# Feature group 2 on seven products for all four chunks, the last attention unit's sums on one engine, and another order in the output projection

## The chip, the cores and the metric

The kernel runs on one core of a Trainium2 chip. Its time is the device time of one execution in microseconds; the median of 3 runs of the kernel before is 745.07 us (744.22 to 745.59). One execution was also profiled, and took 744.5 us. In that profile the engines are called PE (TensorE, its matmuls), PEld (TensorE's weight loads), DVE (VectorE), ACT (ScalarE), POOL (GpSimd) and SP (SyncE, which here only issues transfers). L1190 is line 1190 of the kernel before.

## The reference

A gated layer over 2048 positions of 640 features. The input is normalised; one branch is attention over a dilated window of eight keys, followed by an output projection; the other is a bilinear unit, whose result goes through a silu and multiplies the first.

```python
B, S, D, F, H = 1, 2048, 640, 1536, 32        # Dh = 20, window W = 8, dilation 2
xn = layernorm(x)
q, k, v = split(xn @ wqkv)                    # 32 heads of 20
idx = pos[:, None] - arange(W) * 2            # masked where negative
attn = softmax(einsum("bhsd,bhswd->bhsw", q, k[idx]) * Dh ** -0.5)
s = einsum("bhsw,bhswd->bhsd", attn, v[idx]) @ wo
h = (xn @ w_gate) * (xn @ w_up)               # no nonlinearity on either branch
out = x + s * silu(h @ w_down)
```

## The kernel before

Every product is in single precision, made of three matmuls: each operand is split into a high part (a copy on ACT, L114) and a low part (a subtraction on POOL or DVE, L115), and high x high, high x low and low x high are summed in a bank of PSUM. The normalised input stands transposed in SBUF as four chunks of 512 positions (`xT`, tiles `xc`), and the 1536 features of the bilinear unit are twelve groups of 128.

The program goes through these stages. Products for q, k and v (`qkv`, L433) in blocks of heads, with attention's units following on DVE and POOL. Then feature groups 2 to 11 of the bilinear unit, while attention goes on. Then the output projection, and last the product with `w_down`. Each engine works through its own list in program order, so an instruction that waits holds up all that is behind it on its engine. The order is written out by hand: attention is a generator, and each call of `advance` after a piece of TensorE's work lets it emit as many of its pieces as the piece has credit for.

**Feature groups.** The gate and up products of one feature group over two chunks can be done as a Strassen-like scheme of seven products instead of eight (`group`, L1334): sums of blocks of the weights (S1, S2, S3, S4, d5, on POOL) meet blocks of the input (A11 and so on name the weights' blocks, B11, B21, B22 the input's) and sums of those, T1 to T4. For the chunks 2 and 3 the T tiles are made in SBUF during the q, k, v products (`differences`). For the chunks 0 and 1 they were made at the start and put away in DRAM (`t_scr`, `e_scr`), and come back by `load_t` (L1190, four loads of 768 KB) and `load_e` (L1194, two loads of 512 KB, over the first two rows of chunk 1), all issued from POOL's queue. `F_TWO` is the first feature group whose chunks 0 and 1 use them: 3. So group 2 does the chunks 2 and 3 by seven products, and the chunks 0 and 1 by plain products (`gate` and `up`, L124, 15 matmuls each). From group 3 to 10 each feature group is two calls of `group`. Within a call the products come in the order B11, B21, T2, T1, T3, B22, T4; ACT copies four of them into tiles `gh` (`hold`, L1303), and gate_b (L1306), up_b (L1309), h_b (L1312), gate_a (L1316) and up_a (L1319) combine them; `VEC` = 3 says from which group on up_b and h_b of the chunks 2 and 3 go to DVE instead of POOL. A tile `gh` comes free when its store to `h_scr` has landed; there are six.

**Attention's sums.** A unit has eight terms t = e * v on DVE (L503) and seven additions of them into o (L509), on POOL. Only in the last unit every second addition is on DVE.

**The last h.** `up` multiplies gate and up on DVE (L1378); the very last one is a copy on ACT (L1380) and a product on POOL (L1381). Its store is the last to `h_scr` ahead of the output projection, whose own `gh` tiles are laid where the old ones were.

**The output projection.** Five pairs of blocks of 128 positions by seven products each (`pair_product`, L1041), in the banks A, C, A, C, A, B, A; then six blocks by plain products (L124). ACT holds the products 0, 1 and 2 of a pair in `kept` (L1044); DVE adds product 3 (L1047), product 4 (L1050) and product 5 (L1052) to what was held. Product 6 goes on in bank A after product 4 has been read by L1050. Between them lie the splits of the next pair's input: `hi_pair` (L1016, ACT) and `lo_pair` (L1020, DVE). DVE also transposes blocks of o (L718) and makes sums of `w_down`'s blocks (L805, L808, L814, L817), whose splits run on ACT and POOL.

Of the kernel before, what the change touches and what calls it, by code (L numbers as in the profile page):

```python
# [13 lines left out]
AF = mybir.ActivationFunctionType  # L14
# [28 lines left out]
SP = 10  # L43
PAIRS = range(0, W, 2)
PACE = 1.0
VEC = 3
EARLY = 1
GROUP_RATE = 0.184

# [7 lines left out]
def kernel(  # L57
# [319 lines left out]

    UN = [(g, r) for g in range(len(GROUPS)) for r in range(DIL)]
    ORDER = [0, 1, 2, 3, 4, 6, 5, 7, 8, 11, 9, 10]
    wide, now = [], [None]  # L380
    q_t, kv_t, kv_buf, kv_zero, scr, staged, made = {}, {}, {}, {}, {}, [], set()

    def view_kv(u, b):
# [41 lines left out]
    def qkv(m, r, i, runs=ALL_RUNS, at=None, act=None, bank=("q", 3)):  # L425
# [9 lines left out]
        if m or r:  # L435
            if not staged:
                y = slot([P, 2, 2 * 3 * CMAX], F32)
                staged.extend([y[:, 0], y[:, 1], st([P, 2 * 3 * CMAX], "pk", 1)])
# [27 lines left out]
    def attention():  # L466
# [28 lines left out]
        def values(w):  # L495
# [6 lines left out]
            v = flat(kv_t[u][:, 1, w:w + NE, :]).rearrange("p (n d) -> p n d", d=DH)  # L502
            nc.vector.tensor_mul(t.rearrange("p (n d) -> p n d", d=DH),  # L503
                                 e[:, :, w].unsqueeze(2).to_broadcast([P, NE * nh, DH]), v)
# [866 lines left out]
    def up(f, ch, gs):  # L1371

        p = plain(f, 1, ch)

        def finish():
            hs = st([P, CH], "gh", 5)
            if (f, ch) != (f1, NCH - 1):
                nc.vector.tensor_mul(hs, p, gs)  # L1378
# [9 lines left out]
    def next_sums(f):  # L1388
        w_split(f, "S", "R")
        w_sum.pop(f)  # L1390
        if f < f1:
            load_wf(f + 1)

    def first_parts():
        for name in ("S1", "S2", "S3", "d5", "S4"):
            w_add(2, name)
            yield
        w_split(2, "S")
        yield
        w_split(2, "G")  # L1400
        yield

    steps += [differences(k) for k in range(2)]
# [3 lines left out]
    for m, t in ((m, t) for m in range(1, len(MADE)) for t in range(DIL)):  # L1407
# [3 lines left out]
        for i in range(NE):  # L1411
# [7 lines left out]
            if (m, r, i) == (last - 1, 1, 6):  # L1419
                load_wf(2)  # L1420
            qkv(m, r, i)
            if i == 1:
                finish_piece()
            advance(PACE * heads * 0.38)
# [29 lines left out]
                  (1, 2): splits("G"), (1, 4): splits("S"), (1, 5): splits("R"), (1, 6): splits("U")}  # L1454

    def load_late(n):
        if n < 2:
            load_t(n + 2)
        else:
            load_e(1, n - 2, n - 2)  # L1460

    for f in range(2, f1):
        places.clear()
        if not two(f):
            places.update({(0, 3): sums("S1", "S2"), (0, 4): sums("S3", "d5", "S4")})
# [6 lines left out]
            if two(f + 1):  # L1472
                tw.pop("G")
            w_split(f + 1, "G")
            up(f, 0, g0)
            up(f, 1, g1)
            if two(f + 1):
                tw.pop("U")
            continue
        places.update(two_places)  # L1480
        if f == F_TWO:
            places.update({(0, n): lambda f, n=n: load_late(n) for n in range(4)})
        group(f, 2)
        group(f, 0, 1)
    places.clear()
# [54 lines left out]
    pair_product(0, 0)  # L1540
    for p in range(SP // 2):
        more = p + 1 < SP // 2
        if not more:
            y1 = turn_o(SP)
        if p < 3:
            wd_sums()
        pair_product(p, 1)
# [14 lines left out]
        if more:  # L1562
            if p == 3:
                hi_pair(p + 1, 2)
            if p:
                lo_pair(p + 1, 2)
# [118 lines left out]
```

## Time and profile before

| what | value |
|---|---|
| median of 3 runs | 745.07 us |
| the profiled execution | 744.5 us |
| its span, first to last instruction | 742.7 us |
| PE busy | 734.2 us (99%) |
| DVE busy | 612.5 us (82%) |
| POOL busy | 463.5 us (62%) |
| ACT busy | 301.9 us (41%) |
| granted TensorE clock | 0.999 |

A view of the timeline has a row for each run of like instructions: start, length, engine, line, operation, what it writes and reads, how many; in brackets stands how long the engine was idle ahead of it and what ended that. The execution is 1.8 us longer than its span.

### The profile page before, as it was taken

To read this page: it belongs to the slowest core of one execution; us is meant where nothing else is said; L and a number is where in the kernel's file an instruction comes from. 1 tells how busy PE (TensorE), PEld (TensorE's weight loads), DVE (VectorE), ACT (ScalarE), POOL (GpSimd) and SP (SyncE) were. 2 spreads that over 40 slices of the span, in tenths; PEclk is the share of its full clock that TensorE was granted. 3 is DMA by queue.
4 is the path that set the end of the run, shared out by engine and by line. 5 is a ranking of instruction groups with operands and counts; after the bars stand their busy time and mean duration, and the time that the engine had idled before them with its cause. 6 is when DMAs were issued, how large, how long until landed. Compare 5 with 4: busy or idle time off the path is not lost. (4 is left out here: it accounts for less than half of the span.)

```text
span 742.7 us, 11094 instructions
## 1 busy us (share of the span) xinstructions
PE 734.2 (99%) x4054; PEld 669.7 (90%) x4054; DVE 612.5 (82%) x720; ACT 301.9 (41%) x577; POOL 463.5 (62%) x389
## 2 busy tenths in 40 slices
PE   9999999999999999999999999999999999999997
PEld 7989989988999998888888888888899999999997
DVE  7676998799687988999999998758898777777775
ACT  5668312322332332233232332235556564444442
POOL 6159919887688879798879889787558800000000
PEclk9999999999999999999999999999999999999999
DMA  8465582868355736863455244269457655555534
GB/s 326 164 202 175 220 268 87 247 212 248 97 175 152 232 105 216 286 193 110 154 132 177 75 123 119 64 180 264 126 160 215 232 218 192 192 192 192 192 107 142
DMA packets 103493, 132.98 MB, mean 179 GB/s; under 512 B 22696, under 2 KB 74404, under 8 KB 103438
## 3 DMA queue, kind: packets, MB, share of 16 engines
q1 hardware_dynamic: 86286, 114.25, 48.4%
q10 hardware_dynamic: 16000, 12.78, 5.3%
q0 software_dynamic: 1152, 5.24, 2.2%
q8 instruction: 32, 0.52, 0.3%
q14 instruction: 23, 0.19, 0.1%
HBM read 83.58 MB, written 47.81 MB: 177 GB/s over the span
## 5 line engine op out<-in xcount | busy, mean ns | idle before, releaser
L509 POOL TENSOR_TENSOR o<-o,t 128x960 f32<-128x960 f32 (+1 forms) x69 | 139.9, 2028 | 15.5 <-DVE t L503 14.2
L503 DVE TENSOR_TENSOR t<-e,kv 128x960 f32<-128x960 f32 (+1 forms) x96 | 99.6, 1039 | 23.3 <-POOL o L509 23.3
L535 DVE TENSOR_TENSOR t<-q,kv 128x1920 f32<-128x1920 f32 (+1 forms) x48 | 92.5, 1927 | 4.1 <-DMA kv<-qkv_scr 4.0
L542 DVE TENSOR_REDUCE lg<-t 128x96 f32<-128x1920 f32 (+1 forms) x48 | 92.3, 1923 | 0.2
L433 PE MATMUL q<-s,xc 128*128 128x360 f32 (+1 forms) x450 | 83.0, 334 | 0.0
L115 POOL TENSOR_TENSOR s<-wraw,s 128x384 fp32r<-128x384 f32 (+6 forms) x58 | 69.9, 1215 | 20.0 <-ACT s L114 18.5
L433 PEld LDWEIGHTS q<-s,xc 128*128 128x128 f32 x450 | 75.0, 188 | 4.1 <-POOL s L115 0.4
L1303 ACT ACTIVATE gh<-g 128x512 f32<-128x512 f32 x54 | 32.3, 598 | 109.9 <-PE g L1334 108.9
L433 PE MATMUL u<-s,xc 128*128 128x360 f32 (+1 forms) x360 | 65.7, 334 | 0.0
L433 PEld LDWEIGHTS u<-s,xc 128*128 128x128 f32 x360 | 60.2, 188 | 2.3
L433 PE MATMUL g<-s,xc 128*128 128x360 f32 (+1 forms) x330 | 61.5, 337 | 0.0
L433 PEld LDWEIGHTS g<-s,xc 128*128 128x128 f32 x330 | 55.7, 188 | 2.6
L904 PE MATMUL q<-xc,s 128*128 128x320 f32 x342 | 55.5, 309 | 0.0
L1334 PE MATMUL g<-s,s 128*128 128x512 f32 x216 | 54.8, 389 | 0.0
L1334 PE MATMUL u<-xc,s 128*128 128x512 f32 x216 | 54.8, 389 | 0.0
L904 PEld LDWEIGHTS q<-xc,s 128*128 128x128 f32 x342 | 51.5, 188 | 0.0
L1334 PEld LDWEIGHTS u<-xc,s 128*128 128x128 f32 x216 | 40.5, 188 | 8.5
L1334 PEld LDWEIGHTS g<-s,s 128*128 128x128 f32 x216 | 40.5, 188 | 8.4
L114 ACT ACTIVATE s<-wraw 128x384 fp32r<-128x384 f32 (+6 forms) x59 | 33.6, 588 | 31.1 <-PE g L1334 9.8
L509 POOL TENSOR_TENSOR o<-t 128x960 f32<-128x960 f32 (+1 forms) x12 | 24.4, 2036 | 28.4 <-DVE t L503 26.5
L1334 PE MATMUL g<-xc,s 128*128 128x512 f32 x168 | 41.3, 390 | 0.2 <-ACT gh L1303 0.2
L124 PE MATMUL g<-xc,s 128*128 128x512 f32 (+1 forms) x180 | 40.1, 373 | 0.0
(367 smaller groups left out, 1567.8 us busy)
## 6 DMA issues: line engine op xcount, KB each, us to landing
h_scr<-gh SPq DMA_DIRECT2D x48, 256.0 KB, 2.6
wraw<-in_wgu SPq DMA_DIRECT2D x11, 640.0 KB, 4.3
kv<-qkv_scr SPq DMA_DIRECT2D x14, 480.0 KB, 5.8
t<-h_scr SPq DMA_DIRECT2D x8, 768.0 KB, 7.8
qkv_scr<-s ACTq DMA_DIRECT2D x16, 360.0 KB, 3.6
kv<-qkv_scr SPq DMA_DIRECT2D x14, 367.5 KB, 6.5
s_scr<-gh SPq DMA_DIRECT2D x16, 320.0 KB, 4.1
gh<-s_scr SPq DMA_DIRECT2D x16, 320.0 KB, 3.9
```

Source lines behind the costliest of these rows:

```text
L114: nc.scalar.activation(hi, raw, AF.Copy)
L115: eng.tensor_sub(lo, raw, hi.bitcast(F32))
L124: nc.tensor.matmul(acc, a, b, start=first and n == 0, stop=last and n == len(runs) - 1)
L433: nc.tensor.matmul(p, xT[(r * NE + i) // TPC][a][:, k, t0:t0 + P], wq[m][b][k], start=n == 0, stop=n == len(runs) - 1, skip_group_check=ac ...
L503: nc.vector.tensor_mul(t.rearrange("p (n d) -> p n d", d=DH), e[:, :, w].unsqueeze(2).to_broadcast([P, NE * nh, DH]), v)
L509: return NE * c * cost, lambda: eng.tensor_add(y, z, t)
L535: nc.vector.tensor_mul(t, q, k)
L542: nc.vector.tensor_reduce(out=lg[:, :, j:j + 2].rearrange("p n a -> p a n"), in_=t.rearrange("p a (n d) -> p a n d", d=DH), op=ALU.add, ax ...
L904: nc.tensor.matmul(p, y[:, i, k], wd_t[name][k][:, l], start=new and r == 0, stop=r == len(runs) - 1, skip_group_check=True)
L1303: nc.scalar.activation(kept[j], b["ACACABA"[j]], AF.Copy)
L1334: nc.tensor.matmul(y, w, x, start=j in (0, 1, 5) and r == 0, stop=r == len(runs) - 1, skip_group_check=True)
```

## The change

Four things. Group 2 uses seven products for all four chunks (`F_TWO` = 2, and with it `VEC` = 2); the branch for plain products in the loop, and `next_sums`, fall away. For that the T tiles are loaded earlier: `load_t(0)` among the last q, k, v products, and the others and `load_e` in group 2's first call. A slot for the first load comes free because group 2's high and low weights G move to the buffer `pk`, which the staging of q, k and v gives up seven products ahead of its end. Second, all additions of the last attention unit are on DVE. Third, the last h is multiplied on DVE like the others. Fourth, in the output projection `lo_pair(p + 1, 2)` stands behind product 4 instead of ahead of it for the pairs 1 to 3, and the transpose of the first plain block, `y1`, stands ahead of the sums of `w_down` at the end of pair 3 instead of behind them.

```diff
-VEC = 3
+VEC = 2
...
-            eng, cost = (nc.gpsimd, 1.3e-3) if u != ORDER[-1] else (nc.gpsimd, 2.2e-3) if w % 2 else (nc.vector, 2.5e-3)
+            eng, cost = (nc.gpsimd, 1.3e-3) if u != ORDER[-1] else (nc.vector, 2.5e-3)
...
-    F_TWO = 3
+    F_TWO = 2
...
             hs = st([P, CH], "gh", 5)
-            if (f, ch) != (f1, NCH - 1):
-                nc.vector.tensor_mul(hs, p, gs)
-            else:
-                nc.scalar.activation(hs, p, AF.Copy)
-                nc.gpsimd.tensor_mul(hs, hs, gs)
+            nc.vector.tensor_mul(hs, p, gs)
...
             qkv(m, r, i)
+            if m == last and n == NT - 7:
+                staged[:] = [y for y in staged if y is not stage_pk[-1]]
+            elif m == last and n == NT - 5:
+                load_t(0)
+            elif m == last and n == NT - 3:
+                w_split(2, "G")
...
     def load_late(n):
-        if n < 2:
-            load_t(n + 2)
+        if n == 0:
+            load_t(1)
+            load_t(2)
+        elif n == 1:
+            load_t(3)
         else:
-            load_e(1, n - 2, n - 2)
+            load_e(1, 0, 0)
+            load_e(1, 1, 1)
...
-        if not two(f):
-            places.update({(0, 3): sums("S1", "S2"), (0, 4): sums("S3", "d5", "S4")})
-            if two(f + 1):
-                places.update({(0, 0): lambda f: load_t(0), (0, 2): lambda f: load_t(1)})
-            group(f, 2)
-            next_sums(f + 1)
-            g0 = gate(f, 0)
-            g1 = gate(f, 1)
...
-            up(f, 0, g0)
-            up(f, 1, g1)
...
     for p in range(SP // 2):
         more = p + 1 < SP // 2
-        if not more:
-            y1 = turn_o(SP)
...
             hi_pair(p + 1, 1)
         pair_product(p, 4)
         wd_splits()
-        if not p:
-            lo_pair(1, 2)
         if more:
+            lo_pair(p + 1, 2)
             lo_pair(p + 1, 1)
...
             if p == 3:
                 load_o(SP + 3, 3, st([P, 3, D], "t", 2))
+                y1 = turn_o(SP)
             wd_sums()
```

POOL's list where the q, k, v products end and group 2 begins; o is attention's, `pk` and `s` are split weights, and the DMA rows are `load_t`. Before:

```order
L115 TENSOR_TENSOR s_2478<-wraw_2226,s_2478 128x640
L509 TENSOR_TENSOR o_2430<-t_941 128x640
L509 TENSOR_TENSOR o_2430<-o_2430,t_941 128x640 x6
L115 TENSOR_TENSOR s_2634<-wraw_2292,s_2634 128x384
L115 TENSOR_TENSOR s_2641<-wraw_2226,s_2641 128x640
L1190 DMA s_2652<-t_scr 128x1536
L1190 DMA s_2680<-t_scr 128x1536
```

The same place in the change (lines are one higher there; the rows with `xc` are `load_e`):

```order
L510 TENSOR_TENSOR o_2430<-o_2430,t_941 128x640
L1191 DMA s_2539<-t_scr 128x1536
L510 TENSOR_TENSOR o_2430<-o_2430,t_941 128x640 x2
L115 TENSOR_TENSOR pk_2586<-wraw_2226,pk_2586 128x640
L510 TENSOR_TENSOR o_2430<-o_2430,t_941 128x640 x3
L115 TENSOR_TENSOR s_2636<-wraw_2292,s_2636 128x384
L115 TENSOR_TENSOR s_2636<-wraw_2226,s_2636 128x384
L1191 DMA s_2653<-t_scr 128x1536
L1191 DMA s_2655<-t_scr 128x1536
L1191 DMA s_2668<-t_scr 128x1536
L1195 DMA xc_452<-e_scr_112 128x1024
L1195 DMA xc_452<-e_scr_113 128x1024
```

The split of G moved behind four of the unit's seven additions, the second weight split is narrower, and five loads follow each other where two stood.

DVE's list in pair 1 of the output projection, from the addition of product 3 to that of product 5. Before:

```order
L1047 TENSOR_TENSOR gh_4693<-o_4550,u_4666 128x320
L1020 TENSOR_TENSOR kv_4250<-s_4462,kv_4250 128x768
L1050 TENSOR_TENSOR gh_4707<-o_4550,e_70 128x320
L1020 TENSOR_TENSOR pk_4696<-s_4638,pk_4696 128x640
L1052 TENSOR_TENSOR gh_4693<-o_4550,g_4721 128x320
```

In the change:

```order
L1048 TENSOR_TENSOR gh_4687<-o_4544,u_4660 128x320
L1051 TENSOR_TENSOR gh_4700<-o_4544,e_70 128x320
L1021 TENSOR_TENSOR kv_4245<-s_4457,kv_4245 128x768
L1021 TENSOR_TENSOR pk_4689<-s_4632,pk_4689 128x640
L1053 TENSOR_TENSOR gh_4687<-o_4544,g_4715 128x320
```

The addition of product 4 comes ahead of the wide low part; the two low parts still stand ahead of the addition of product 5. Pairs 2 and 3 change alike.

DVE's list in the change where the last h is now multiplied, between the sums of pair 1's input and the first sums of `w_down`:

```order
L994 TENSOR_TENSOR s_4481<-s_4481 128x256
L1378 TENSOR_TENSOR gh_4539<-u_4523,gh_4521 128x512
L806 TENSOR_TENSOR lg_4561<-wraw_4492 128x320
L809 TENSOR_TENSOR lg_4562<-wraw_4492,lg_4561 128x320
L1021 TENSOR_TENSOR xc_4542<-s_4481,xc_4542 128x640
L1048 TENSOR_TENSOR gh_4593<-o_4544,u_4565 128x320
```

The row L1378 is new here; before, L805 followed L993 directly.

More of the change, by code (lines that the diff above doesn't have):

```diff
@@ L379 @@
     ORDER = [0, 1, 2, 3, 4, 6, 5, 7, 8, 11, 9, 10]
-    wide, now = [], [None]
+    wide, now, stage_pk = [], [None], []
     q_t, kv_t, kv_buf, kv_zero, scr, staged, made = {}, {}, {}, {}, {}, [], set()
@@ L437, in qkv @@
                 y = slot([P, 2, 2 * 3 * CMAX], F32)
-                staged.extend([y[:, 0], y[:, 1], st([P, 2 * 3 * CMAX], "pk", 1)])
+                stage_pk.append(st([P, 2 * 3 * CMAX], "pk", 1))
+                staged.extend([y[:, 0], y[:, 1], stage_pk[-1]])
             if c > CMAX and not wide:
@@ L1386, in up @@
         advance(PACE * 2.8)
[L1388 to L1392, printed above, removed]
     def first_parts():
@@ L1398, in first_parts @@
         w_split(2, "S")
-        yield
-        w_split(2, "G")
         yield
@@ L1456, in load_late @@
     def load_late(n):
-        if n < 2:
-            load_t(n + 2)
-        else:
-            load_e(1, n - 2, n - 2)
+        if n == 0:
[3 more added lines that the diff above has]
+            load_t(3)
+        else:
+            load_e(1, 0, 0)
+            load_e(1, 1, 1)
     for f in range(2, f1):
         places.clear()
-        if not two(f):
-            places.update({(0, 3): sums("S1", "S2"), (0, 4): sums("S3", "d5", "S4")})
-            if two(f + 1):
-                places.update({(0, 0): lambda f: load_t(0), (0, 2): lambda f: load_t(1)})
-            group(f, 2)
-            next_sums(f + 1)
-            g0 = gate(f, 0)
-            g1 = gate(f, 1)
-            if two(f + 1):
-                tw.pop("G")
-            w_split(f + 1, "G")
-            up(f, 0, g0)
-            up(f, 1, g1)
-            if two(f + 1):
-                tw.pop("U")
-            continue
         places.update(two_places)
         if f == F_TWO:
-            places.update({(0, n): lambda f, n=n: load_late(n) for n in range(4)})
+            for n in range(3):
+                places[0, n] = lambda f, n=n: load_late(n)
         group(f, 2)
@@ L1564 @@
                 hi_pair(p + 1, 2)
-            if p:
-                lo_pair(p + 1, 2)
             hi_pair(p + 1, 1)
```

## The prediction

> **What bounds the kernel now.** I read the page first, then the waits of TensorE, then the timeline at the places that the change touches.
>
> ```profile
> PE 734.2 (99%) x4054; PEld 669.7 (90%) x4054; DVE 612.5 (82%) x720; ACT 301.9 (41%) x577; POOL 463.5 (62%) x389
> ```
>
> TensorE is busy for 734.2 us, 99% of the span, so time is gained only by taking matmuls away or by closing one of its few gaps. In the feature groups its waits are a single one of 0.2 us, behind a hold on ACT:
>
> ```profile
> PE g L1334 <- ACT gh L1303: 0.2, 1, 0.2
> ```
>
> The gaps that count lie in the output projection. They are seen best on the weight loads, which run just ahead of their matmuls:
>
> ```profile
> 529.23 0.88 PEld L1041 LDWEIGHTS q<-xc,kv 128*128 128x128 f32 x6 [1.62 <-DVE gh L1050]
> ...
> 531.78 0.88 PEld L1041 LDWEIGHTS e<-xc,s 128*128 128x128 f32 x6 [0.36 <-ACT o L1044]
> ...
> 538.13 0.88 PEld L1041 LDWEIGHTS e<-xc,xc 128*128 128x128 f32 x6 [0.63 <-DVE gh L1050]
> ...
> 546.43 0.89 PEld L1041 LDWEIGHTS q<-xc,pk 128*128 128x128 f32 x6 [0.38 <-DVE gh L1050]
> ...
> 554.74 0.88 PEld L1041 LDWEIGHTS q<-xc,xc 128*128 128x128 f32 x6 [0.39 <-DVE gh L1050]
> ...
> 559.77 0.88 PEld L1041 LDWEIGHTS e<-xc,xc 128*128 128x128 f32 x6 [0.64 <-ACT o L1044]
> ```
>
> The bracket holds the idle time and what ended it. The six sum to 1.62 + 0.36 + 0.63 + 0.38 + 0.39 + 0.64 = 4.02 us. Four wait for L1050, DVE's addition of product 4, ahead of which product 6 may not go on in its bank; two wait for a hold on ACT. So two things can shorten the kernel: group 2's matmuls and these 4.02 us.
>
> What must stay hidden is attention on DVE. After the length of each stretch stand the busy times of PE, PEld, DVE, ACT and POOL:
>
> ```profile
> 300.00:330.00 30.00, 30.00 (x134) 24.82 (x134) 29.39 (x31) 9.68 (x17) 25.42 (x24) 1.00 0.74 228
> 330.00:390.00 60.00, 60.00 (x266) 49.70 (x265) 55.93 (x57) 19.53 (x33) 49.03 (x38) 1.00 0.48 138
> 390.00:450.00 60.00, 59.79 (x264) 49.17 (x263) 57.59 (x51) 19.19 (x32) 54.98 (x40) 1.00 0.38 120
> ```
>
> DVE: 29.39 + 55.93 + 57.59 = 142.91 of 150 us. It has 7.1 us to spare there, no more.
>
> **Part 1, group 2 by seven products.** TensorE's rows:
>
> ```profile
> 272.13 1.52 PE L1334 MATMUL g<-xc,s 128*128 128x512 f32 x6
> ...
> 284.40 3.56 PE L124 MATMUL g<-xc,s 128*128 128x512 f32 x15
> ...
> 294.60 3.56 PE L124 MATMUL u<-xc,s 128*128 128x512 f32 x15
> 298.00 1.52 PE L1334 MATMUL g<-xc,pk 128*128 128x512 f32 x6
> ```
>
> The seven products of the chunks 2 and 3 start at 272.13; the plain ones start at 284.40 (four rows of 15, the first and the last shown) and end at 298.00, where group 3 begins. 60 matmuls take 13.60 us, 0.2267 each. Seven products have 7 x 6 matmuls and 4 x 3 for the fifth block, 54 in all: 12.24 us. **-1.36 us.**
>
> The cover that this needs is the T tiles in time. POOL issues their loads; below its rows stands how long those two took to land:
>
> ```profile
> 274.42 1.56 POOL L509 TENSOR_TENSOR o<-o,t 128x640 f32<-128x640 f32 x1 [0.55 <-DVE t L503]
> 275.95 2.55 POOL L115 TENSOR_TENSOR s<-wraw,s 128x384 fp32r<-128x384 f32 x2
> 278.45 1.30 POOL L1190 DMA_DIRECT2D s<-t_scr  x2
> ```
>
> ```profile
> DMA to landing us min/median/max: 7.4/8.0/8.5
> ```
>
> The last addition ends at 275.98, two weight splits (2.55 us) follow, and the two loads go at 278.45. With the second issued 0.65 us after the first (half of 1.30), and 7.4 and 8.5 us to landing, it landed 1.75 us behind it: my price for 768 KB in a filled queue, and 1.2 for 512 KB. In the change the same work stands ahead of them but for a second split of 384 columns instead of 640 (2.55 x 768 / 1024 = 1.9 us for both), so the run of loads starts near 278.0; the first tile was fetched during the q, k, v products. Landing: 285.4, 287.1 and 288.9 for the T tiles, 290.1 and 291.3 for `load_e`. Needed, counting 0.2267 from 284.40: T2's high part after 15 matmuls at 287.8, its low part at 288.25, T3's second row at 291.4, T4 at 294.6 and 295.05. The tightest has 1.1 us to spare. I take 0; the other end is 2 us, if POOL comes 3 us later than before. The five loads fill POOL's queue for about 3.2 us where 1.3 stood; behind them wait attention's additions and group 3's sums of weights, which POOL can make up, with 30 - 25.42 = 4.6 us free in the stretch from 300. The split of G, now among the additions, is due at 272.13 behind the last product but two; were it late, TensorE would wait for what is left of it, at most the length of such splits, 2.55 us. I take 0.
>
> The Trainium skill speaks against these loads: SBUF — State Buffer, section SBUF: two separate sides, says that transfers issued from GpSimd's queue can starve while VectorE holds the port pair that the two share. On the other hand the Trainium skill's DMA: Bandwidth & Descriptors, section Anatomy of one DMA, gives 2.0 us plus bytes over 436 GB/s, about 3.8 us for one T tile; by that the loads are far from the path. The landing row, 7.4 to 8.5 us beside a busy DVE, is nearer to the first.
>
> On DVE, group 2 gets up_b and h_b of the chunks 2 and 3, and three operations instead of two for the others: three more of 0.7 to 2 us, some 3 of its 7.1 us to spare. 0 for TensorE; what they cost without that cover is the fourth rival.
>
> **Part 2, the last unit's sums.** An addition on DVE, POOL's last one of that unit, and the first transpose of the output projection:
>
> ```profile
> L509 DVE TENSOR_TENSOR o<-o,t x3: 1157/1522/1953, 464.9 to 479.1; 128x960 f32<-128x960 f32 x3
> ```
>
> ```profile
> 481.99 2.26 POOL L509 TENSOR_TENSOR o<-o,t 128x960 f32<-128x960 f32 x1 [2.94 <-DVE t L503]
> ```
>
> ```profile
> 503.48 1.56 DVE L718 STREAM_TRANSPOSE wraw<-kv 128x640 f32<-128x640 f32 x2
> ```
>
> Four more additions of 1.2 to 1.95 us are 5 to 8 us more on DVE, and the unit's waits for POOL fall away. It ended at 484.25, and what it makes is transposed at 503.48, 19 us later. 0 for TensorE. Since all later pieces of attention move by half a step in the order, a hold may wait more or less behind an exp on ACT: between -0.2 (the wait above) and +0.5.
>
> **Part 3, the last h on DVE.** DVE, SP, and the landing of stores to `h_scr` around there:
>
> ```profile
> 520.84 1.80 DVE L993 TENSOR_TENSOR s<-s 128x256 f32<-128x256 f32 x1
> ...
> 528.29 0.49 DVE L1047 TENSOR_TENSOR gh<-o,u 128x320 f32<-128x320 f32 x1 [2.31 <-DMA h_scr<-gh]
> 528.69 0.48 DVE L1050 TENSOR_TENSOR gh<-o,q 128x320 f32<-128x320 f32 x1
> ...
> 530.70 0.48 DVE L1052 TENSOR_TENSOR gh<-o,g 128x320 f32<-128x320 f32 x1
> ```
>
> ```profile
> 524.92 0.38 SPq L1292 DMA_DIRECT2D h_scr<-gh  x1
> ```
>
> ```profile
> DMA to landing us min/median/max: 2.7/2.9/3.1
> ```
>
> L1047 needs a tile that lies where the last h lay, and waited 2.31 us for its store, from 525.98. SP issues it at 524.92, when POOL's product is done; DVE goes on 3.37 us later, at 528.29, L1050 follows at 528.69, and TensorE at 529.23. In the change DVE multiplies at 522.57, when L993 is through. The price is that of the like operation, 0.69 us:
>
> ```profile
> L1378 DVE TENSOR_TENSOR gh<-g,gh x2: 681/686/692, 296.9 to 513.7; 128x512 f32<-128x512 f32 x2
> ```
>
> So the store goes at 523.3, and L1047 may start at 526.67. DVE's operations ahead of it end 0.69 us later than 525.98, also at 526.67. L1050 ends 0.88 us later, at 527.55. TensorE's wait began at 529.23 - 1.62 = 527.61. It is gone: **-1.62 us**; if the store or DVE is 0.8 later, -0.8.
>
> **Part 4, the order of sums.** Pair 1 on DVE, the holds on ACT that wait for L1052, and TensorE's next product in the bank of the second hold:
>
> ```profile
> 536.23 1.45 DVE L1020 TENSOR_TENSOR kv<-s,kv 128x768 fp32r<-128x768 f32 x1
> 537.60 0.47 DVE L1050 TENSOR_TENSOR gh<-o,e 128x320 f32<-128x320 f32 x1
> ...
> 539.00 0.47 DVE L1052 TENSOR_TENSOR gh<-o,g 128x320 f32<-128x320 f32 x1
> ```
>
> ```profile
> 531.29 0.44 ACT L1044 ACTIVATE o<-e 128x320 f32<-128x320 f32 x1 [5.28 <-DVE gh L1052]
> ...
> 539.59 0.44 ACT L1044 ACTIVATE o<-q 128x320 f32<-128x320 f32 x1 [2.60 <-DVE gh L1052]
> ```
>
> ```profile
> 540.43 1.04 PE L1041 MATMUL q<-xc,kv 128*128 128x320 f32 x6
> ```
>
> With L1050 ahead of the 1.45 us low part, the waits of 0.63, 0.38 and 0.39 at product 6 end. But DVE's timeline has no idle bracket from 528.29 to 557.79, and L1052 still comes behind both low parts. The hold of the next pair's product 0 waits for L1052 (2.60 us), since it overwrites what L1052 reads. It ends at 540.03, and TensorE uses its bank at 540.43: 0.40 us of slack. So of 1.40 us the first 0.40 can be kept, and the rest reappears as a wait for that hold. I take **-0.35 us**, between 0 and -1.40. The wait of 0.36 at 531.78 has the same cause and stays.
>
> The last gap, 0.64 us at 559.77, comes from the transpose of y1 at 557.79, behind the sums of `w_down` from 556.02:
>
> ```profile
> 556.02 0.77 DVE L805 TENSOR_TENSOR lg<-wraw 128x320 f32<-128x320 f32 x1
> ...
> 557.79 0.83 DVE L718 STREAM_TRANSPOSE s<-t 128x640 f32<-128x640 f32 x1
> ```
>
> ```profile
> 558.66 0.74 ACT L744 ACTIVATE xc<-s 128x640 fp32r<-128x640 f32 x1 [0.92 <-DVE s L718]
> ```
>
> ACT's split waits for it, and the hold of product 2 waits behind that split. Ahead of the two sums the transpose starts 1.77 us earlier, more than the gap: **-0.6 us**, between 0 and -0.64.
>
> **The sum.** -1.36 - 1.62 - 0.35 - 0.6 = -3.93 us. The profiled execution took 744.5 us, 1.8 more than its span; it would take 740.6. The median of the runs is 0.57 above it: 745.07 - 3.9 = **741.2 us**.
>
> **Rivals.**
>
> *The gaps close wholly.* If DVE gets faster with less of POOL beside it, all 4.02 us go: 745.07 - 1.36 - 4.02 = 739.7 us. Against it stands DVE without idle time.
>
> *The projection gives back.* DVE is its bound, and the gain is only what its restart moves by, 0.8 us at the worse end above: 745.07 - 1.36 - 0.8 = 742.9 us. For it: L993 takes 1.80 us where L1050, wider, takes 0.48, so operations there can stretch.
>
> *The T tiles come late.* From a POOL 1.1 us late on, TensorE waits at T2. If it is 3 us late and part 4 then gains nothing, 741.2 + 1.9 + 0.95 = 744.0 us, which can't be told from no change. For it: five loads in a row; against it the 1.1 to 4.5 us to spare.
>
> *DVE falls behind in attention: slower.* The tiles `gh` are a ring of six. A row of up_a, and one of the hold that takes the same tile again:
>
> ```profile
> 411.61 0.67 DVE L1319 TENSOR_TENSOR gh<-gh,g 128x512 f32<-128x512 f32 x1
> ```
>
> ```profile
> 415.16 0.60 ACT L1303 ACTIVATE gh<-u 128x512 f32<-128x512 f32 x1 [0.81 <-PE u L1334]
> ```
>
> up_a ends at 412.28; its store needs 2.7 to 3.1 us, so it lands near 415.1, and the hold starts at 415.16. When DVE is late there is nothing to spare. DVE gets some 3 us more at group 2 and TensorE 1.36 less to hide it in. The Trainium skill's SBUF — State Buffer, section SBUF: two separate sides, has an operation of VectorE with two inputs in SBUF and one of GpSimd block each other whole, which would stretch DVE's extra sums further. If DVE then stays 0.5 us later at 14 of the 16 calls of `group` from 3 to 10, TensorE loses 7 us: 745.07 - 3.9 + 7 = 748.2 us. It decides from a lag of 0.1 us at that call. Against it: before, so late a DVE cost TensorE no more than the 0.2 us above.
>
> **How the numbers follow.** Forecast 0.52; all gaps closed 0.12; projection gives back 0.15; late tiles 0.10; slower 0.11. A measurement of this kernel can tell 0.2%, 1.5 us, from no change. Faster by more: 0.52 + 0.12 + 0.15 less 0.02 = 0.77. Within: 0.12. Slower: 0.11. The range, 739.6 to 744.3 us, holds all but the slower case and the edges; the likeliest case alone is 740.4 to 742.2.
>
> **What would show it.** Group 2's two calls should last 24.5 us together, with no wait of TensorE at T2. L1047's wait of 2.31 us should be under 0.3 and TensorE's wait for L1050 in the first pair gone, while the holds behind L1052 show short waits in the pairs 2 to 4 instead. Waits of TensorE for L1303 of over 0.5 us in sum would speak for the slower rival; a wait for a load from `t_scr`, for late tiles. The forecast is wrong if the projection's waits still sum to more than 2.2 us, or if group 2 takes over 25 us.

## The result, and the profile after

The change makes the kernel 0.5% faster: 742.41 us median of 22 runs (741.37 to 745.85) against 745.42 us of the kernel before on the same chip (744.22 to 748.61). The ratio is 0.9952, with a 95% interval of 0.994 to 0.9963. The forecast was 741.2 us, with a range of 739.6 to 744.3. The profiled execution took 742.42 us, and its span is 740.0 us instead of 742.7. Its lines are one higher than before's from L439 on, so that the addition of product 5, L1052 before, is L1053 now.

The page's line of busy times, TensorE first:

```profile
PE 732.1 (99%) x4048; PEld 667.8 (90%) x4048; DVE 625.0 (84%) x728; ACT 302.5 (41%) x578; POOL 454.3 (61%) x384
```

TensorE has 2.1 us less to do (734.2 before) and is still busy for 99% of the span; DVE has 12.5 us more, POOL 9.2 less.

TensorE's timeline at group 2, in the profile of the change: its first call, its second call, and the start of group 3.

```profile
272.15 1.52 PE L1335 MATMUL g<-xc,pk 128*128 128x512 f32 x6
...
284.39 1.52 PE L1335 MATMUL g<-xc,pk 128*128 128x512 f32 x6
...
296.63 1.52 PE L1335 MATMUL g<-xc,pk 128*128 128x512 f32 x6
```

The two calls take 24.48 us, 1.39 less than the 25.87 before, and there is no bracket in them: no wait for a T tile.

TensorE's weight loads with a wait in the feature groups, in the same profile:

```profile
376.77 0.19 PEld L1335 LDWEIGHTS u<-xc,s 128*128 128x128 f32 x1 [0.39 <-POOL s L115]
...
454.33 1.93 PEld L1335 LDWEIGHTS g<-xc,s 128*128 128x128 f32 x9 [0.58 <-ACT gh L1304]
...
508.93 3.31 PEld L124 LDWEIGHTS g<-xc,s 128*128 128x128 f32 x15 [0.28 <-DVE gh L1320]
```

1.25 us in sum, where the kernel before had 0.64 (for a hold, at 418.73) and 0.15 (ahead of the last gate). The prediction's single wait of 0.2 us in the groups was counted on the matmuls; counted on the weight loads, as here and as in the projection, it is these 0.79. The wait for the hold L1304 is 0.58 against 0.64, so it does not speak for the slower rival.

Its weight loads with a wait in the output projection:

```profile
529.46 0.88 PEld L1042 LDWEIGHTS e<-xc,s 128*128 128x128 f32 x6 [0.58 <-ACT o L1045]
...
537.78 0.88 PEld L1042 LDWEIGHTS q<-xc,kv 128*128 128x128 f32 x6 [0.40 <-ACT o L1045]
...
546.18 0.88 PEld L1042 LDWEIGHTS q<-xc,s 128*128 128x128 f32 x6 [0.48 <-ACT o L1045]
...
554.50 0.88 PEld L1042 LDWEIGHTS e<-xc,s 128*128 128x128 f32 x6 [0.41 <-ACT o L1045]
```

1.87 us in sum instead of 4.02. No wait for the addition of product 4 is left and none for the transpose of y1. All four are of one kind: they wait for ACT's hold of the next pair's first product. DVE and ACT in pair 1 show where that comes from; first DVE:

```profile
534.30 1.05 DVE L1021 TENSOR_TENSOR kv<-s,kv 128x768 fp32r<-128x768 f32 x1
535.28 1.50 DVE L1021 TENSOR_TENSOR pk<-s,pk 128x640 fp32r<-128x640 f32 x1
536.70 0.47 DVE L1053 TENSOR_TENSOR gh<-o,g 128x320 f32<-128x320 f32 x1
```

And ACT's hold:

```profile
537.29 0.44 ACT L1045 ACTIVATE o<-q 128x320 f32<-128x320 f32 x1 [2.62 <-DVE gh L1053]
```

L1053, the addition of product 5, comes behind both low parts (L1021). The hold overwrites what L1053 reads and waits 2.62 us for it; then TensorE waits 0.40 us for the hold's bank.

The other sign, that L1047's wait would be under 0.3 us, was not met. L1048, the same addition in the change:

```profile
525.14 0.49 DVE L1048 TENSOR_TENSOR gh<-o,u 128x320 f32<-128x320 f32 x1 [1.09 <-ACT xc L114]
```

It still waits 1.09 us, most likely for the store, although the bracket names ACT: the store was issued at 522.31 and took 2.5 us to land, and L1048 follows the landing by 0.33 us, as this addition does by 0.27 to 0.31 us in the kernel before, in e1, e3 and e7 again. DVE got there sooner than I had worked out, since the two sums of `w_down` ahead of it took 0.57 and 0.49 us instead of 1.17 and 1.47. TensorE has no wait for it any more.

By stretches of the profile, from one start on TensorE to the next, all in microseconds. "Groups" is from group 3 to the first product of the output projection. Runs of one kernel spread by 1 to 7 us, more than most of these differences, so the experiments are read from these stretches first and from the medians second.

| kernel | group 2 | groups | projection | span | median | ratio to before, 95% interval |
|---|---|---|---|---|---|---|
| before | 25.87 | 222.23 | 70.01 | 742.7 | 745.42 | 1 |
| the change | 24.48 | 222.67 | 67.87 | 740.0 | 742.41 | 0.9952 (0.994 to 0.9963) |
| e1, part 1 alone | 24.48 | 224.42 | 69.47 | 743.1 | 744.99 | 0.998 (0.9963 to 0.9997) |
| e2, all but part 1 | 25.86 | 222.79 | 67.81 | 741.1 | 743.74 | 0.9971 (0.9953 to 0.9988) |
| e3, last h as before | 24.53 | 223.27 | 68.66 | 741.5 | 744.50 | 0.9976 (0.996 to 0.9992) |
| e4, low parts as before | 24.52 | 222.53 | 68.13 | 740.5 | 742.23 | 0.9955 (0.9941 to 0.997) |
| e5, y1 as before | 24.48 | 222.13 | 68.74 | 740.5 | 743.10 | 0.9971 (0.9957 to 0.9984) |
| e6, last unit's sums as before | 24.50 | 224.00 | 67.88 | 747.0 | 744.02 | 0.9983 (0.9966 to 1.0) |
| e7, a low part behind product 5 | 24.51 | 222.21 | 66.00 | 740.0 | 740.32 | 0.9922 (0.9897 to 0.9947) |
| e7 again | 24.48 | 222.54 | 66.00 | 738.1 | 740.35 | 0.9923 (0.9904 to 0.9943) |
| e8, T tiles later | 26.74 | 222.59 | 67.88 | 742.1 | 744.58 | 0.9986 (0.9974 to 0.9999) |
| e10, e7 with `VEC` = 3 | 24.48 | 222.50 | 66.00 | 738.0 | 741.73 | 0.9951 (0.993 to 0.9971) |

Between the two profiles the 2.7 us come about so: group 2 -1.39, groups +0.44, projection -2.14, the product with `w_down` +0.05, the tail behind the last five products +0.32 (7.58 instead of 7.26), the start +0.02. Programs that are alike in the groups measured 222.1 to 223.3 there, and all tails lie between 7.24 and 7.67, so neither +0.44 nor +0.32 can be put down to the change by these two profiles alone.

### The profile page after: what moved, and what is told of

Read it like the earlier page. It is cut to its first block, busy times and chain, and to the rows that moved or that the text cites. A ratio compares the mean times of both kernels' runs of the same rounds, so it can differ in the third digit from the quotient of the medians.

```text
span 740.0 us, 11087 instructions
## 1 busy us (share of the span) xinstructions
PE 732.1 (99%) x4048; PEld 667.8 (90%) x4048; DVE 625.0 (84%) x728; ACT 302.5 (41%) x578; POOL 454.3 (61%) x384
## 4 chain that ended last, share of the span: by engine, by line
PE 94%; DMA 2%; DVE 1%; POOL 1%; issue 1%; ACT 1%; SPq 0%; ACTq 0%; DVEq 0%; POOLq 0%
PE g L1335 15%; PE q L433 10%; PE u L1335 10%; PE q L905 9%; PE u L433 8%; PE g L433 8%; PE u L905 6%; PE q L1335 5%; PE g L124 5%; PE u L124 5%; PE g L905 3%; PE e L905 3%; PE q L124 2%; PE e L433 1%; PE e L124 1%; PE q L1042 1%
## 5 line engine op out<-in xcount | busy, mean ns | idle before, releaser
L510 POOL TENSOR_TENSOR o<-o,t 128x960 f32<-128x960 f32 (+1 forms) x66 | 133.2, 2019 | 10.2 <-DVE t L504 9.4
L1304 ACT ACTIVATE gh<-g 128x512 f32<-128x512 f32 x57 | 34.1, 599 | 113.5 <-PE g L1335 109.7
L1335 PE MATMUL u<-xc,s 128*128 128x512 f32 x228 | 58.1, 390 | 0.0
L1335 PE MATMUL g<-s,s 128*128 128x512 f32 x228 | 57.9, 389 | 0.0
L1335 PEld LDWEIGHTS u<-xc,s 128*128 128x128 f32 x228 | 42.8, 188 | 9.3 <-POOL s L115 0.4
L1335 PEld LDWEIGHTS g<-s,s 128*128 128x128 f32 x228 | 42.8, 188 | 8.8
L1335 PE MATMUL q<-xc,pk 128*128 128x512 f32 x171 | 41.8, 389 | 0.0
L510 POOL TENSOR_TENSOR o<-t 128x960 f32<-128x960 f32 (+1 forms) x11 | 22.1, 2011 | 28.9 <-DVE t L504 27.1
```

The source lines that it names most:

```text
L510: return NE * c * cost, lambda: eng.tensor_add(y, z, t)
L1304: nc.scalar.activation(kept[j], b["ACACABA"[j]], AF.Copy)
L1335: nc.tensor.matmul(y, w, x, start=j in (0, 1, 5) and r == 0, stop=r == len(runs) - 1, skip_group_check=True)
```

## The experiments

### e1_group_only: part 1 alone

```diff
-VEC = 3
+VEC = 2
...
-    F_TWO = 3
+    F_TWO = 2
...
+            elif m == last and n == NT - 5:
+                load_t(0)
```

with the rest of part 1; everything else as in the kernel before.

> Part 1 alone: group 2 by seven products with its loads and splits; the last unit's sums, the last h and the projection stay as before. If the steps are independent, group 2 takes 24.5 us instead of 25.9 and the six waits of the projection stay at about 4.0 us in sum: the span falls by 1.4 us, from 742.7 to 741.3. Rival (what group 2 adds on VectorE comes back as waits in the groups 3 to 10): the new waits there sum to 0.7 us or more and the span is 742.0 or longer.

Measured: group 2 gains its 1.39 us, but the groups behind it take 224.42 us, 2.19 more than before, and the span is 743.1, no shorter than before. The runs still put it 0.2% ahead (0.998). Five waits on TensorE's weight loads, 3.33 us in sum, stand there where the kernel before had two of 0.79 together (0.35 us of the increase ran under matmuls still going on). The longest:

```profile
476.77 0.19 PEld L1335 LDWEIGHTS u<-xc,s 128*128 128x128 f32 x1 [1.53 <-POOL s L115]
```

The wait of 1.53 us is for a split of weights on POOL. POOL in that run, up to that split (the last row, which ends at 476.72):

```profile
463.88 2.26 POOL L510 TENSOR_TENSOR o<-t 128x960 f32<-128x960 f32 x1 [1.19 <-DVE t L504]
...
471.33 2.26 POOL L510 TENSOR_TENSOR o<-o,t 128x960 f32<-128x960 f32 x1
...
474.79 1.93 POOL L115 TENSOR_TENSOR s<-wraw,s 128x384 fp32r<-128x384 f32 x1
```

Two of attention's additions (L510) stand ahead of it, 2.26 us each. They stand ahead of this split in the kernel before too, where it is this row:

```profile
474.57 1.01 POOL L115 TENSOR_TENSOR s<-wraw,s 128x384 fp32r<-128x384 f32 x1
```

There it ended at 475.58, some 0.6 us before TensorE came to it. In e1 it ended 1.14 us later, most of it because the split itself took 1.93 us instead of 1.01, and TensorE came about 1 us earlier; the two make up the 0.6 to spare and the wait of 1.53. The same split in the change, where the last unit's additions are on DVE:

```profile
471.28 1.93 POOL L115 TENSOR_TENSOR s<-wraw,s 128x384 fp32r<-128x384 f32 x1
```

There it ends at 473.21, and TensorE has no wait. So the rival of this run held: part 1 alone gives back its gain in the groups. It suggests that part 2, the last unit's sums, which I had priced at 0, is what keeps the gain; e6 tests that.

### e2_rest_only: the other parts without part 1

```diff
-                nc.scalar.activation(hs, p, AF.Copy)
-                nc.gpsimd.tensor_mul(hs, hs, gs)
+            nc.vector.tensor_mul(hs, p, gs)
...
-            if p:
-                lo_pair(p + 1, 2)
...
+            lo_pair(p + 1, 2)
```

with the last unit's sums and y1 as in the change; group 2 as before.

> Parts 2 to 4 without part 1: group 2 keeps its plain products. If the steps are independent, the projection goes from 70.0 to 67.9 us and its waits from 4.0 to 1.9; the span falls by 2.1 us, from 742.7 to 740.6. Rival (the projection's gain hangs on the earlier end of the feature groups): the projection stays over 69 us.

Measured: projection 67.81 us, -2.20, as expected; it does not hang on group 2. The groups are 0.56 longer than before, with three waits for POOL's splits (0.39, 0.24 and 0.63) and one for a hold. The longest and the one for the hold, on the weight loads:

```profile
403.28 0.19 PEld L1334 LDWEIGHTS u<-xc,s 128*128 128x128 f32 x1 [0.63 <-POOL s L115]
...
419.31 1.91 PEld L1334 LDWEIGHTS g<-xc,s 128*128 128x128 f32 x9 [0.25 <-ACT gh L1303]
```

The span is 741.1 instead of the expected 740.6, by these waits. They can't be put down to part 2: all four stand at 299 to 420 us, and up to about 461 us POOL's list is that of the kernel before. In this execution POOL waited 2.22 us instead of 1.70 for weights to be loaded ahead of its first sum of weights behind the two `t_scr` loads (281.96 instead of 281.45), and its list stayed 0.5 to 1.1 us later. Where part 2 acts, near 476 us, the kernel before has no wait of TensorE that it could take away, and e2 has none either.

### e3_h_as_before: the last h back on ACT and POOL

```diff
-            nc.vector.tensor_mul(hs, p, gs)
+            if (f, ch) != (f1, NCH - 1):
+                nc.vector.tensor_mul(hs, p, gs)
+            else:
+                nc.scalar.activation(hs, p, AF.Copy)
+                nc.gpsimd.tensor_mul(hs, hs, gs)
```

> The change with the last h back on ScalarE and GpSimd. My theory: VectorE's addition of product 3 in the first pair waits some 2.3 us again for the store of that h, and TensorE's product 6 of that pair some 1.6 us for the addition of product 4; the waits behind the holds stay. Span 741.6 instead of 740.0. Rival (the new order of low parts already took that wait away): within 0.3 us of 740.0.

Measured: the wait came back, but smaller. DVE's addition of product 3 in the first pair:

```profile
527.54 0.49 DVE L1048 TENSOR_TENSOR gh<-o,u 128x320 f32<-128x320 f32 x1 [1.71 <-POOL kv L115]
```

And TensorE's weight loads:

```profile
528.48 0.89 PEld L1042 LDWEIGHTS q<-xc,kv 128*128 128x128 f32 x6 [1.02 <-DVE gh L1051]
...
531.03 0.88 PEld L1042 LDWEIGHTS e<-xc,s 128*128 128x128 f32 x6 [0.34 <-ACT o L1045]
```

TensorE waits 1.02 us for the addition of product 4, not 1.62, and then 0.34 for the hold, where the change waits 0.58 once. The projection is 68.66 us, 0.79 longer than the change's. The bracket of L1048 names POOL's split, but the store of h was issued at 524.77 and took 2.5 us to land, until 527.27, and L1048 followed 0.27 us later, about as in every other run; so the store is the likelier cause. The span of 741.5 is near what I expected, but 0.60 of the difference stands in the groups, whose program is the change's. e1 has the kernel before's program in the projection and shows the same, 1.10 us at product 6:

```profile
529.60 0.88 PEld L1042 LDWEIGHTS q<-xc,kv 128*128 128x128 f32 x6 [1.10 <-DVE gh L1051]
```

So the 1.62 us of the profile before was on the high side for that program: there the store took 3.1 us to land, and L1047 followed its issue by 3.37 us (524.92 to 528.29); in e1 and e3 the store took 2.5 us, and e3 shows 527.54 - 524.77 = 2.77.

### e4_low_as_before and e5_y1_as_before: the two parts of the order

e4 takes the low part 2 back ahead of product 4, e5 the transpose of y1 to the start of pair 4.

```diff
+            if p:
+                lo_pair(p + 1, 2)
...
-            lo_pair(p + 1, 2)
```

> The change with the low parts 2 of the pairs 2 to 4 back ahead of product 4's addition. My theory: the waits behind the hold in those pairs (0.40 + 0.48 + 0.41 = 1.29 us) turn back into the waits for the addition of product 4 that the kernel before had there (0.63 + 0.38 + 0.39 = 1.40 us), so that this order bought 0.1 us: projection 68.0 us instead of 67.9, span 740.1. My prediction had 0.35 for it (projection 68.2). Rival (the order buys all that it removes): projection 69.2 us.

Measured for e4:

```profile
529.81 0.89 PEld L1042 LDWEIGHTS e<-xc,s 128*128 128x128 f32 x6 [0.73 <-ACT o L1045]
...
536.16 0.89 PEld L1042 LDWEIGHTS e<-xc,xc 128*128 128x128 f32 x6 [0.63 <-DVE gh L1051]
...
544.47 0.89 PEld L1042 LDWEIGHTS q<-xc,pk 128*128 128x128 f32 x6 [0.38 <-DVE gh L1051]
...
552.77 0.88 PEld L1042 LDWEIGHTS q<-xc,xc 128*128 128x128 f32 x6 [0.39 <-DVE gh L1051]
```

In the later pairs the three waits for the hold turned into three for L1051, with the very numbers of the kernel before: 0.63 + 0.38 + 0.39 = 1.40 us instead of 0.40 + 0.48 + 0.41 = 1.29. The projection is 68.13 us, 0.26 longer; 0.11 of it is this exchange, 0.15 the first wait (0.73 instead of 0.58), whose program is the change's, so that this part is spread between executions. The waits only changed their place, as expected.

```diff
+        if not more:
+            y1 = turn_o(SP)
...
-                y1 = turn_o(SP)
```

> The change with the transpose of y1 back at the start of pair 4, behind the sums of w_down. My theory: ScalarE's split and the hold behind it are late again, and TensorE waits 0.6 us near 557: projection 68.5 us, span 740.6. Rival (with less waiting ahead of it VectorE reaches that transpose in time anyway): no wait there, projection 67.9.

Measured for e5: the wait is back, with 0.86 us, and the projection is 0.87 longer.

```profile
557.00 0.89 PEld L1042 LDWEIGHTS e<-xc,xc 128*128 128x128 f32 x6 [0.86 <-ACT o L1045]
```

### e6_sums_as_before: half of the last unit's sums back on POOL

```diff
-            eng, cost = (nc.gpsimd, 1.3e-3) if u != ORDER[-1] else (nc.vector, 2.5e-3)
+            eng, cost = (nc.gpsimd, 1.3e-3) if u != ORDER[-1] else (nc.gpsimd, 2.2e-3) if w % 2 else (nc.vector, 2.5e-3)
```

> The change with half of the last unit's additions back on GpSimd. What I predicted of this part was 0: span 740.0, the stretch from group 3 to the projection 222.2 to 223.3 us. My theory now, from the run of part 1 alone, which had a wait of 1.53 us at 476.8 for a split of weights on GpSimd: two additions of 2.26 us stand ahead of that split, and with TensorE some 1.4 us earlier than in the kernel before they make it late. That wait comes back here with 1.2 to 1.8 us: the stretch takes 224.0 to 224.6 us, the span is 741.4 or more.

Measured: the same wait at the same matmul as in e1, 1.53 us again, and groups of 224.00 us, where the runs of the change's other variants have 222.1 to 222.7 and once 223.3.

```profile
482.47 0.19 PEld L1335 LDWEIGHTS u<-xc,s 128*128 128x128 f32 x1 [1.53 <-POOL s L115]
```

The span says nothing here: that execution lost 5.9 us ahead of group 2, where nothing differs (last section). The median, 744.02, is 1.6 above the change's. What I predicted of part 2, 0, falls: beside part 1 it is worth about 1.5 us (1.33 in the groups, a wait of 1.53, 1.6 in the medians). Without part 1 there is no wait at that matmul, in the kernel before or in e2, so there it can gain nothing at that place.

### e7_low_behind_p5: what bounds the projection now

```diff
-            lo_pair(p + 1, 1)
         pair_product(p, 5)
+        if more:
+            lo_pair(p + 1, 1)
```

> The change with one line moved: the low part 1 of the next pair comes behind product 5's addition on VectorE instead of ahead of it. It is needed only at product 4 of the next pair. If the four waits that are left (0.58 + 0.40 + 0.48 + 0.41 = 1.87 us) come from the hold that must wait for that addition, they go nearly all: span 738.2, projection 66.1 us. Rival (VectorE is the bound of the projection whatever the order): the wait only moves to the additions of products 3 and 4 of the next pair, and the span falls by less than 0.6 us.

Measured: projection 66.00 us, 67.87 - 1.87: all four waits are gone. That profile's span was 740.0 nevertheless, since it reached group 2 at 274.42 instead of 272.15, so the kernel was run again.

> The same kernel as e7_low_behind_p5 once more: its profile had lost 2.3 us ahead of group 2, where its program does not differ from the change's, without a wait. If that was a matter of that execution, this profile shows group 2 starting near 272.2 as in the change, the projection again 66.0 us, and a span of 737.5 to 738.5 us; the ratio to the kernel before stays near 0.992. If the moved line itself costs time ahead of group 2, the span is 740 again.

The second profile reaches group 2 at 272.30, has 66.00 us in the projection again and a span of 738.1. Its windows row from 520 to 560 (length, then the busy times of PE, PEld, DVE, ACT and POOL with their counts, the clock, the share of the DMA engines and GB/s):

```profile
520.00:560.00 40.00, 40.00 (x275) 40.00 (x274) 37.64 (x63) 24.52 (x54) 24.58 (x21) 1.00 0.64 172
```

The change in the same window:

```profile
520.00:560.00 40.00, 39.18 (x262) 38.13 (x261) 38.38 (x61) 23.97 (x53) 22.40 (x20) 1.00 0.61 166
```

TensorE is busy for all 40.00 us, and DVE, with 37.64, less than in the change. DVE in pair 1:

```profile
534.93 0.47 DVE L1053 TENSOR_TENSOR gh<-o,g 128x320 f32<-128x320 f32 x1
535.33 1.10 DVE L1021 TENSOR_TENSOR pk<-s,pk 128x640 fp32r<-128x640 f32 x1
```

L1053 now stands between the two low parts, ahead of the one that is needed only at product 4 of the next pair. Twice the kernel stands at 0.992 of the one before, with 740.3 us, some 2 us below the change's median, as the projection's 1.87 us would have it.

### e8_t_later: the price of late T tiles

```diff
-            for n in range(3):
-                places[0, n] = lambda f, n=n: load_late(n)
+            places[0, 5] = lambda f: (w_add(f + 1, "S1"), [load_late(n) for n in range(3)])
```

> The change with the last three loads of T tiles and both loads of e behind GpSimd's first sum of weights in group 2: issued near 283.6 instead of 277.7, 5.9 us later. It prices the rival of late tiles. With the 1.1 us to spare that I worked out, TensorE waits 4 to 5 us at the first product that needs them (287.8), the span is 744 to 745 us. Rival (the tiles land so early that GpSimd may be late by much more than I said): a wait under 2.5 us, span below 742.5.

The three loads, in POOL's timeline, and the waits of TensorE that follow:

```profile
283.50 1.63 POOL L1191 DMA_DIRECT2D s<-t_scr  x3
```

```profile
288.50 0.30 PEld L1335 LDWEIGHTS g<-s,s 128*128 128x128 f32 x2 [1.04 <-issue]
290.30 0.76 PEld L1335 LDWEIGHTS g<-s,s 128*128 128x128 f32 x4 [1.50 <-DMA s<-t_scr]
```

5.8 us later (283.50 instead of 277.71) cost 1.04 + 1.50 = 2.54 us on the weight loads, and group 2 takes 26.74 us, 2.26 more. The difference of some 3.5 us is not what the change has to spare, since the loads landed faster here: the second tile in 6.2 us instead of 9.6 (last section), so at 290.26, only 2.4 us later than the change's 278.27 + 9.57 = 287.84. The rows of e8 show that two weight loads of T2 go with the first tile and the rest with the second. TensorE's weight loads for T2 in the change:

```profile
287.57 1.32 PEld L1335 LDWEIGHTS g<-s,s 128*128 128x128 f32 x6
```

The third of these six goes at about 288.02. So 0.2 us were to spare in the change, where I had worked out 1.1, and 2.4 - 0.2 = 2.2 is about what e8 lost. The result lies at the rival's border of 2.5 and 742.5 us, and far from the 4 to 5 us that I expected.

### e10_low_vec3: which engine sets the groups' waits

```diff
-VEC = 2
+VEC = 3
```

on e7.

> e7_low_behind_p5 with the up sum and the product of h of the chunks 2 and 3 of group 2 on GpSimd instead of VectorE. It asks which engine sets the waits of the feature groups. If it is VectorE, which is late after the work that part 1 gave it (the rival by which the change would be slower), then the stretch from group 3 to the projection gets shorter by 0.3 to 1 us. If it is GpSimd's splits of weights (the wait of 0.39 us at 376.8), two more operations of 1.3 us there change nothing or add waits in group 3: the stretch stays at 222.1 to 223.3 us or gets longer.

Measured: 222.50 us in the groups, and the three waits stand where the change has them, each within 0.1 us of it; the first two:

```profile
376.72 0.19 PEld L1335 LDWEIGHTS u<-xc,s 128*128 128x128 f32 x1 [0.30 <-POOL s L115]
...
454.25 1.92 PEld L1335 LDWEIGHTS g<-xc,s 128*128 128x128 f32 x9 [0.56 <-ACT gh L1304]
```

DVE has 2.1 us less work from 272.1 to 300 us there than in e7 again (24.50 instead of 26.58 busy), and that changed nothing in these waits, so that work is not what TensorE waits for. The medians, 741.73 and 740.35, don't tell the two apart, as their intervals overlap.

## Why the prediction was right, and where it was not

**The bound.** Right: time came only from matmuls that fell away and from the projection's waits.

**Part 1.** The term -1.36 measured -1.39, and the T tiles came in time, but by 0.2 us, not by the 1.1 that I worked out (e8): they took 8.5 and 9.6 us to land instead of 7.4 and 8.5. That this 0 held is luck. POOL did make up the loads put into its queue: its next three splits into `pk` start at 291.06, 315.77 and 339.61, before at 296.90, 318.39 and 340.98. Wrong was the 0 for what follows: I had not asked what a TensorE that comes 1.4 us earlier meets in the lists of the other engines 180 us behind group 2. Attention is later there. The reduction with which the last unit's sums are prepared, before:

```profile
454.82 0.56 DVE L569 TENSOR_REDUCE sm<-e 128x48 f32<-128x384 f32 x1 [0.62 <-ACT e L564]
```

And in the change:

```profile
458.68 0.55 DVE L570 TENSOR_REDUCE sm<-e 128x48 f32<-128x384 f32 x1
```

Attention is 3.9 us later there, while TensorE is about 1 us earlier (group 2's 1.39 us less what it waited since). This is not the lag at group 2 that my rival had in mind. The same reduction of the earlier units stands at 337.20 in the change and at 338.42 before, so attention is not late 45 us behind group 2; it is later by 1.0 at 378.38, by 1.3 at 418.57, and by 3.9 at the last, where two sums of the feature group, of 0.68 and 2.70 us, stand ahead of it on DVE that came behind it before. And e10, with 2.1 us less work on DVE at group 2, has this reduction at 458.59 all the same. What makes attention fall back between 338 and 459 us, the order of its pieces or something else, stays open. In e1 the groups lost 2.19 us, not the 7 us of my rival and not mainly in the place that I gave it: the longest wait, 1.53 of 3.33 us, was for a split on POOL that ended 1.14 us later than before, for a TensorE that came about 1 us earlier.

**Part 2.** I predicted 0 and meant nothing to be hidden by it. In the change it is worth about 1.5 us (e6), since it takes the last unit's additions out of POOL's queue ahead of that split. So two of my zeros were wrong with opposite signs, and that they nearly cancel is luck: part 1 and part 2 make -1.39 + 0.44 = -0.95 us for the feature groups by these two profiles, where I had -1.36.

**Part 3.** The mechanism was right for TensorE: its wait behind the last store is gone. DVE's wait for it is not, 1.09 us are left where I expected under 0.3; e7 again has 1.25 there and no wait of TensorE in the projection, so it costs nothing. The term of -1.62 was too large. Between the two profiles the first pair's waits fell by 1.40 us (from 1.62 + 0.36 to 0.58), and by e3 the move is worth 0.79. The 1.62 came from one execution in which the store landed late (e1, with the same program there, has 1.10), and part of what ends is waited for right behind it: the hold of the first pair waits 0.58 us now instead of 0.36. My own lower end of 0.8 was the better price.

**Part 4.** The slack of 0.40 us behind the hold was read rightly: of the 1.40 us, 1.29 came back as waits for the hold, so the three later pairs gained 0.11, not 0.35; e4 gives 0.26 in all, of which 0.15 is spread. y1 was worth 0.64 by the profile before and 0.87 by e5, against 0.6. Together the projection gained 2.14 us where I had 2.57.

**The sum.** -3.93 was forecast between the profiles; they show -2.7, and the medians -3.0. Of the 1.2 us that are missing, 0.43 lie in the projection (0.22 in the first pair, 0.24 in the later ones, where y1 gave 0.04 more), 0.44 in the groups and 0.32 in the tail. The first is a term that was too large, the second three waits of which no run shows whether they are the change's making or the spread between executions, the third not of the change's making as far as the runs show.

**The rivals.** "The gaps close wholly" had against it that DVE was without idle time. That argument was wrong: e7 closes all of them with the same work on DVE in another order. DVE was not the bound there, the order of its list was. "The projection gives back" did not come. Late tiles did not come either, by 0.2 us. Nor did the slower case: e1 is not slower than the kernel before (0.998); it shows 2.19 us lost in the groups, mostly by POOL's splits and not by the ring of `gh`.

## What to carry to other kernels

When TensorE gets earlier, something that was just ready in time may not be any more: follow the list of every engine that has to keep up with it, to its end, before you price that at 0. Here the wait came some 180 us behind the place of the change (e1). An engine without idle time is not yet the bound: ask which of its results someone waits for, and whether what stands ahead of that result is needed later. And price a wait on several executions, since one that ends on a transfer may be half a microsecond too long in the one that was profiled.

## What the runs showed of the hardware

**A slower stretch of matmuls at full clock.** In the first profile of e7 the products for q, k and v from about 195 to 274 us ran slower than in the change, without any wait. Two rows of TensorE in the change:

```profile
252.95 2.56 PE L433 MATMUL u<-s,xc 128*128 128x360 f32 x15
255.35 2.56 PE L433 MATMUL q<-s,xc 128*128 128x360 f32 x15
```

And in that profile of e7:

```profile
252.22 2.63 PE L433 MATMUL g<-s,xc 128*128 128x360 f32 x15
254.69 2.63 PE L433 MATMUL u<-s,xc 128*128 128x360 f32 x15
```

15 matmuls take 2.40 us in the one and 2.47 in the other, 0.160 against 0.1645 us each, while the windows give a granted clock of 1.00 for both. Over the stretch that is the 2.3 us by which group 2 came late. The profile of e6 has the same pace there, and in addition a granted clock of 0.97 and 0.95 in its first 40 us, and loses 5.9 us in all ahead of group 2. The other profiles have neither. Matmuls of 512 columns kept their 0.2267 us, but for the first six of group 2 in these two profiles, which took about 0.23. What sets this pace stays open; it is one source of the spread between runs of one kernel.

**What a load from POOL's queue waits for.** In the prediction I put the 7.4 to 8.5 us of the T tiles nearer to the rule of the Trainium skill's SBUF — State Buffer, section SBUF: two separate sides, by which transfers that GpSimd issues can starve while VectorE holds the port pair that the two share. In the change three T tiles took this long to land:

```profile
DMA to landing us min/median/max: 8.5/9.6/10.9
```

In e8 the same three, issued 5.8 us later:

```profile
DMA to landing us min/median/max: 4.9/6.2/7.7
```

The windows in which they were issued and moved, in the change:

```profile
278.00:280.00 2.00, 2.00 (x10) 1.65 (x10) 2.00 (x3) 0.60 (x1) 2.00 (x5) 1.00 0.94 260
...
286.00:288.00 2.00, 2.00 (x10) 1.67 (x9) 2.00 (x4) 0.60 (x1) 2.00 (x3) 1.00 1.09 421
```

And in e8:

```profile
282.00:284.00 2.00, 2.00 (x10) 1.65 (x10) 2.00 (x3) 0.00 (x0) 2.00 (x3) 1.00 0.06 15
284.00:286.00 2.00, 2.00 (x11) 1.65 (x10) 2.00 (x3) 0.06 (x1) 2.00 (x5) 1.00 0.67 117
```

DVE is busy for 2.00 of 2.00 us in all of them, so how busy it is doesn't make the difference. What differs is the DMA engines: they were filled when the change issued its loads (share 0.94 and 260 GB/s from 278), and nearly idle ahead of e8's (0.06 from 282). The first tile of e8 took 4.9 us, 1.1 more than the estimate of 3.8 us worked out in the prediction from the Trainium skill's DMA: Bandwidth & Descriptors, section Anatomy of one DMA; the two loads behind it shared the DMA engines with it. So with the fp32 sums and reductions that DVE ran there, the starving that the first of the two pages tells of is not seen: 421 GB/s were moved from 286 to 288 beside a DVE that was never idle. The landing went with what the DMA engines had to move already.
